# A planned job order for a one-core attention and MoE kernel: TensorE's instruction transfers and neighbour-dependent times enter the planner, and the search is replayed from a list of seeds

## The chip, the cores and the metric

The kernel runs on one core of a Trainium2 chip. The metric is the device time of one execution in microseconds (us), the median of several runs of the kernel before: 524.87 us, from 524.27 to 526.25.

## The reference: what is computed

Three blocks follow each other, in float32, for batch 4, sequence 576, model width 512.

```python
# 1. attention, 8 heads of 64: heads 0-3 see a local window of 32, heads 4-7 every 32nd position
scores = where(mask[h], q @ k.T / 8, -1e9);  attn = softmax(scores);  x = attn @ v
# 2. channel mixing: xk, xr are mixes of x and x shifted by one position
k = max(xk @ w_k, 0);  v = (k * k) @ w_v;  r = sigmoid(xr @ w_r);  x = r * v
# 3. gated feed-forward with a width-3 convolution over the sequence
h = max(x @ w_in, 0);  c = conv3(h);  out = (h * sigmoid(c)) @ w_out
```

## The kernel before

**Precision and counts.** Every large product is made of three matmuls on rounded parts (high by high, low by high, high by low), each of 128 x 288 or 128 x 512 columns. In the profile these are `mm` at L719 (channel mixing, 1,920 matmuls), `hh` at L977 (w_in, 672) and `oo` at L1045 (w_out, 432). Attention is made of small matmuls: scores `sc` at L524, transposes `tr` at L568 and L578, values `pv` and `tr` at L601 and L610. One attention unit is one batch, one pair of heads and one half of the sequence: there are 32. The first batch has four wide local units; all others are narrow.

**Two stages, two plans.** The work up to the end of channel mixing is one list of jobs, the last block is a second one. A job (`plan.add`) names the engine or engines that may run it with a planned duration for each, the buffers that it reads and writes, and a function that issues its instructions. `Plan.run` is a list scheduler. It keeps for each engine a time at which it is free, takes again and again the job that could start first (ties go to the higher `rank`, the length of the path behind it), adds its duration, and so fixes the order of instructions on TensorE, VectorE (DVE), ScalarE (ACT), GpSimd (POOL) and of the DMA issues on SyncE (SP). On the chip each engine works in that fixed order and waits on semaphores; the planned times themselves are not used there, with one exception below.

**The search.** `Plan.search` runs the scheduler 300 times. Each time it draws, from one random stream with seed 1, a window of time and a share of the jobs in it, changes their rank and, for jobs that may run on ACT or DVE, a lean to one of them, and keeps the change when the planned end of TensorE's last job is not later. Then it runs the best order once more, and that order is issued.

**What the planner knows of TensorE.** A job costs its planned duration, plus `ENTER` 0.21 us when the job before it was not a score or value job and this one is, plus `LEAVE` 0.25 us the other way. It also follows how fast the queue ahead of TensorE fills: `FEED` is 14.2 ns for one instruction, `QUEUE` 64 instructions may wait ahead, and a job is not over before its instructions have been fed (`filled`).

**Stirring.** Up to 60 us of the first stage, where the plan leaves TensorE idle for long enough, dummy matmuls on a zero tile (`stir`, L886) are issued into a bank that is free or about to be overwritten. Ten stand at the start. Their number is worked out from the planned idle time: `int((start - pe_end - 0.3) / 0.17)`. This is the exception: planned times decide a number of instructions.

Of the kernel before, what the change touches and what calls it, by code (L numbers as in the profile page):

```python
# [30 lines left out]
DMA_RATE, DMA_LATENCY = 280.0e3, 2.0  # L31
FOREVER = 1.0e9
PREFER, PREFER_FROM, BESIDE = 0.5, 20.0, 0.3
ENTER, LEAVE = 0.21, 0.25
QUEUE, FEED = 64, 0.0142
ROUNDS = 300
HALF_ARRAY = {"sc", "pv"}
BLOCKS = ("B11", "B21", "B22", "T4", "T1", "T2", "T3")
WEIGHTS = ("A11", "A12", "A22", "S3", "S4", "S1", "S2")
# [3 lines left out]
SECOND = {"PE": 0.0, "ACT": 3.0, "DVE": 4.0, "POOL": 0.0, "SP": 0.0}  # L43
# [24 lines left out]

class Job:
    def __init__(self, n, engines, emit, table, nbytes, fed):  # L70
        self.fed, self.lean = fed, 0.0
        self.n, self.engines, self.emit, self.table, self.nbytes = n, engines, emit, table, nbytes
        self.before, self.after, self.spaces = {}, [], []
        self.rank, self.end, self.done, self.room = 0.0, 0.0, False, None
        self.tail = 0.0


class Plan:
# [5 lines left out]


    def __init__(self):
        self.jobs, self.hints, self.tags, self.opened = [], [], {}, {}

    def add(self, engines, emit, reads=(), writes=(), table=None, nbytes=0, fed=0):
        j = Job(len(self.jobs), engines, emit, table, nbytes, fed)  # L90
        self.jobs.append(j)
        for group, write in ((reads, False), (writes, True)):
            for x in group:
                s, parts = x if isinstance(x, tuple) else (x, range(len(x.writer)))
                if s.place is None:
                    s.place = len(self.tags.setdefault(s.tag, []))
                    self.tags[s.tag].append(s)
                    self.opened.setdefault(s.tag, 0)
                if s not in j.spaces:
                    j.spaces.append(s)  # L100
                    s.left += 1
                    s.jobs.append(j)
                for i in parts if not isinstance(parts, int) else (parts,):
# [61 lines left out]
        for j in self.jobs:  # L165
            j.end, j.done, j.room = 0.0, False, None

    def search(self, start=None, rounds=0):
# [4 lines left out]
        keep = [(j.rank, 0.0) for j in self.jobs]  # L173
        draw, best, at = random.Random(1), None, None
        for k in range(rounds):
            tried = list(keep)
            if at:
                t0, width = draw.uniform(0.0, best), draw.choice((8.0, 25.0, 400.0))
                amount, share = draw.choice((0.3, 1.0, 3.0)), draw.choice((0.05, 0.3))
                for i, j in enumerate(self.jobs):  # L180
                    if abs(at[i] - t0) <= width / 2 and draw.random() < share:
                        rank, lean = tried[i]
                        if len(j.engines) > 1 and draw.random() < 0.5:
                            lean = draw.uniform(-0.6, 0.4)
                        tried[i] = rank + draw.gauss(0.0, amount), lean
            for j, (j.rank, j.lean) in zip(self.jobs, tried):
                pass
            self.reset(opened, spaces)
            out = self.run(start, best)
            end = max(end for _, e, _, end in out if e == "PE") if out else FOREVER  # L190
            if best is None or end <= best:
                best, keep = end, tried
                at = {j.n: t for j, _, t, _ in out}
        if rounds:
            for j, (j.rank, j.lean) in zip(self.jobs, keep):
                pass
        self.reset(opened, spaces)
        return self.run(start, None, True)

    def run(self, start=None, limit=None, final=False):  # L200

        free = dict(start or dict.fromkeys(LATENCY, 0.0))
        dma, table, out, halves, filled = 0.0, None, [], False, 0.0
# [3 lines left out]
        left = len(self.jobs)  # L207

        def release(j):
            for e in j.engines:  # L210
# [1 line left out]
                ready[e].append((t, j))  # L212

        for j in self.jobs:
            j.halves = any(s.tag in HALF_ARRAY for s in j.spaces)
            if not wait[j]:
                release(j)
        while left:
            best, bound = None, FOREVER
            for e, jobs in ready.items():  # L220
                now = free[e]
                for t, j in jobs:
                    if t < now:
                        t = now
                    if t > bound + 1.0:
                        continue
                    for s in j.spaces:
                        if not s.open:
                            t = max(t, self.slot(s, j))
                    if t > bound + 1.0:  # L230
                        continue
                    late = t
                    if e == "DVE" and len(j.engines) > 1:
                        late += j.lean + PREFER * (t > PREFER_FROM)
                    if e == "PE" and j.halves:
                        late += max(0.0, max(filled, t - QUEUE * FEED) + j.fed * FEED - t - j.engines[e]) - BESIDE * halves
                    key = (round(late, 2), -j.rank, j.n)
                    if t < FOREVER and (best is None or key < best[0]):
                        best, bound = (key, t, e, j), late
            assert best, "no job can start"  # L240
            _, t, e, j = best
            if e == "PE" and final:
                j.room = self.room(j, free[e])
            for s in j.spaces:
                if not s.open:
                    s.open = True
                    self.opened[s.tag] += 1
            cost = j.engines[e]
            if e == "PE":
                cost += 0.0 if halves == j.halves else ENTER if j.halves else LEAVE  # L250
                halves = j.halves
                filled = max(filled, t - QUEUE * FEED) + j.fed * FEED
                cost = max(cost, filled - t)
            if j.table and j.table != table:
                cost += 1.29
                table = j.table
# [23 lines left out]
def block_kernel(ctx, tc, qkL, qkS, vL, vW, vS, mu_k, mu_r, w_k, w_v, w_r, w_in, conv_w, w_out, ident, mask_l, mask_w, mask_s, out):  # L280
# [195 lines left out]
    def unit(b, p, half, loaded):  # L476
# [46 lines left out]
                    for u in steps:  # L523
                        pe.matmul(bank_of[j]()[to + u:to + u + m, at_[j]:at_[j] + nk], qk()[r, qo[j] + u:qo[j] + u + m], qk()[r, ko[j] + u:ko[j] + u + nk], start=True, stop=True)  # L524

        cost = 0.06 if local and not wide else 4 * (0.002 + nk * 0.00024) if twist else 0.033 + nk * 0.00167
        if early:
            for s_ in range(2):
                k = plan.add({"PE": len(sections[s_]) * cost}, lambda e, s_=s_: scores(e, sections[s_]), [(qk, range(1 + s_))], [banks[s_]], fed=8 * len(sections[s_]))
                if s_ == 0:  # L530

                    for j in late:
                        j.before[k] = True
                        k.after.append(j)
        else:
            first_scores.append(plan.add({"PE": nb * cost}, lambda e: scores(e, range(nb)), [qk], banks, fed=8 * nb * len(steps)))
        for s_, blocks in enumerate(sections):
            def masked(e, blocks=blocks):
                for i in blocks:
# [32 lines left out]
        else:  # L572
# [4 lines left out]
                for i, n in pairs:  # L577
                    pe.transpose(turned()[:n, i // 2 * rows:(i // 2 + 1) * rows], pr()[:rows, i * gap:i * gap + n], id_sb[:rows, :rows])  # L578

            plan.add({"PE": n0 * (0.108 if local else 0.1) - 0.07}, turn, [pr, fixed["id"]], [turned], fed=2 * n0)  # L580
            both = nb // 2 * rows

            def turned_out(e):
# [25 lines left out]
                            r, o = slice(64 * ab, 64 * ab + 64), i * rows + 64 * (ab ^ (odd and turn_of[1])) + u  # L609
                            pe.matmul(outs_[odd]()[r, i * nq + u:i * nq + u + m], vt()[part, v, r], pt()[part, o:o + m], start=True, stop=True)  # L610

        plan.add({"PE": nb * (0.12 if wide else 0.08 if local else 0.062)}, values, [vt, pt], outs_, fed=8 * nb * len(steps))
        x, n = xT[b], nb * nq
        if wide:
            copy(lambda: x()[:, p, 1 + first * nq:1 + (first + nb) * nq], lambda: out_()[:, :n], n, [out_], [(x, 2 * p + half)])
# [268 lines left out]
    def stir(n, into, anew=True):  # L884
        for _ in range(n):
            pe.matmul(into[:, :T], idle[:, :P], idle, start=anew, stop=anew)  # L886
# [38 lines left out]
        j.tail = TAIL  # L925

    def issue(stirred=False):
        pe_end = 0.0
        with tc.manual_schedule():
            if stirred:  # L930
                stir(WARM, scrap)
            for job, e, start, end in plan.search(START if stirred else SECOND, ROUNDS):
                if e == "PE":
                    if stirred and 5.0 < start < STIR_UNTIL and job.room:
                        bank, anew = job.room
                        n = int((start - pe_end - 0.3) / 0.17)
                        if n > 0:
                            stir(n, bank(), anew)
                    pe_end = end
                job.emit(e)  # L940

    issue(True)
# [231 lines left out]
```

## Time and profile before

| | us |
|---|---|
| median of 3 runs | 524.87 |
| lowest, highest | 524.27, 526.25 |
| the profiled execution | 524.43 |
| its span, first to last instruction | 522.6 |
| TensorE busy | 510.7 (98% of the span) |
| VectorE busy | 390.2 (75%) |
| ScalarE busy | 356.2 (68%) |
| matmuls, and weight loads | 4,898 each |
| DMA moved | 90.27 MB, mean 173 GB/s |

The span is 1.8 us shorter than the profiled execution's time. A busy TensorE is not one at its peak: a matmul's record lasts longer than the distance to the next one's start, and dummy matmuls are busy too. Distances between starts of groups in the timeline tell more than the busy share.

### The profile page before, as it was taken

The numbers are of one execution on the slowest core, as the hardware profiler recorded it, in microseconds if no ns is written. First come the engines' busy times: TensorE is split into PE (matmuls) and PEld (weight loads), VectorE is DVE, ScalarE is ACT, GpSimd is POOL, SyncE is SP. The second block draws the span as 40 slices with busy tenths as digits, with TensorE's granted clock in tenths as the row PEclk, the third lists the DMA queues.
The fourth block names the chain that finished last, engine by engine and source line by source line (L and its number), as shares of the span: only waits on it lengthen the run. The fifth ranks groups of instructions, "written<-read, shape, count | busy, mean of one in ns | idle before, by whom it ended". The sixth has DMA issues, their size and how long they took to land.

```text
span 522.6 us, 12915 instructions
## 1 busy us (share of the span) xinstructions
PE 510.7 (98%) x4898; PEld 474.6 (91%) x4898; DVE 390.2 (75%) x1143; ACT 356.2 (68%) x1074; POOL 1.1 (0%) x15
## 2 busy tenths in 40 slices
PE   9999999999999989999999999999999999999997
PEld 5679999989999979999999999999989898898885
DVE  4989899988957978878887415599986876696610
ACT  5989997999947889949799344376644645455420
POOL 0000000000000000000000000000000000000000
PEclk9989999999999999999999999999999999999999
DMA  7965565995476593478785540754137006300111
GB/s 228 357 243 168 181 204 167 300 299 167 153 254 221 155 342 106 152 249 268 265 300 190 153 142 2 272 188 180 40 102 257 27 16 246 131 21 20 41 41 60
DMA packets 50654, 90.27 MB, mean 173 GB/s; under 512 B 4257, under 2 KB 32673, under 8 KB 50593
## 3 DMA queue, kind: packets, MB, share of 16 engines
q1 hardware_dynamic: 50304, 89.29, 50.8%
q8 instruction: 38, 0.62, 0.5%
q14 instruction: 24, 0.19, 0.1%
q10 hardware_dynamic: 288, 0.16, 0.1%
HBM read 60.80 MB, written 28.64 MB: 171 GB/s over the span
## 4 chain that ended last, share of the span: by engine, by line
PE 90%; DVE 5%; ACT 3%; issue 1%; POOL 0%; DVEq 0%; ACTq 0%; POOLq 0%
PE mm L719 48%; PE oo L1045 19%; PE hh L977 15%; PE sc L524 3%; PE pv L610 2%; PE tr L578 2%; DVE pr L540 1%; DVE c L1024 1%; ACT mx L698 1%; ACT pr L545 1%; PE tr L610 1%; PE scrap L886 0%; DVE pr L556 0%; DVE c L1026 0%; DVE mx L699 0%
## 5 line engine op out<-in xcount | busy, mean ns | idle before, releaser
L977 PEld LDWEIGHTS hh<-x,wi 128*128 128x128 f32 x672 | 92.8, 188 | 3.8 <-DVE c L1026 0.6
L977 PE MATMUL hh<-x,wi 128*128 128x288 f32 x672 | 95.1, 296 | 0.5 <-DVE gAl L1031 0.4
L719 PE MATMUL mm<-X,wvh 128*128 128x288 f32 x448 | 84.1, 298 | 0.0
L719 PE MATMUL mm<-Y,wkh 128*128 128x288 f32 x384 | 68.3, 294 | 0.0
L719 PEld LDWEIGHTS mm<-X,wvh 128*128 128x128 f32 x448 | 66.8, 188 | 0.5
L719 PE MATMUL mm<-Y,wrh 128*128 128x288 f32 x256 | 57.9, 305 | 0.2
L545 ACT ACTIVATE pr<-pr,nmx 128x54 f32<-128x54 f32 (+2 forms) x160 | 53.4, 341 | 5.1 <-DVE nmx L540 4.8
L719 PEld LDWEIGHTS mm<-Y,wkh 128*128 128x128 f32 x384 | 56.6, 188 | 0.1
L1024 DVE SCALAR_TENSOR_TENSOR c<-hb,cw_sb,c 128x576 f32<-128x576 f32 x64 | 50.8, 813 | 0.6
L719 PE MATMUL mm<-X,wvl 128*128 128x288 f32 x224 | 47.9, 295 | 0.0
L719 PEld LDWEIGHTS mm<-Y,wrh 128*128 128x128 f32 x256 | 43.3, 191 | 1.2 <-ACT rs L731 0.6
L1045 PE MATMUL oo<-wo,gAh 128*128 128x512 f32 x160 | 43.2, 392 | 0.0
L719 PE MATMUL mm<-Y,wkl 128*128 128x288 f32 x192 | 40.9, 294 | 0.0
L719 PE MATMUL mm<-Y,wrl 128*128 128x288 f32 x128 | 38.3, 299 | 0.6 <-DVE wrl L401 0.6
L760 DVE TENSOR_TENSOR X<-sq,X 128x288 fp32r<-128x288 f32 x48 | 21.7, 456 | 23.0 <-ACT X L758 19.5
L719 PEld LDWEIGHTS mm<-X,wvl 128*128 128x128 f32 x224 | 35.9, 188 | 0.0
L1045 PE MATMUL oo<-wo,gBh 128*128 128x512 f32 x128 | 34.4, 390 | 0.0
L1025 ACT ACTIVATE c<-c 128x576 f32<-128x576 f32 x32 | 21.9, 686 | 17.6 <-DVE c L1024 17.2
L1045 PEld LDWEIGHTS oo<-wo,gAh 128*128 128x128 f32 x160 | 28.8, 188 | 4.8
L742 ACT ACTIVATE rl<-mm 128x288 f32<-128x288 f32 x64 | 25.4, 405 | 8.8 <-PE mm L719 8.6
L545 ACT ACTIVATION_READ_ACCUMULATOR pr<-pr,nmx 128x1 f32 x160 | 31.2, 195 | 0.0
L719 PEld LDWEIGHTS mm<-Y,wkl 128*128 128x128 f32 x192 | 30.7, 188 | 0.0
(121 smaller groups left out, 1056.4 us busy)
## 6 DMA issues: line engine op xcount, KB each, us to landing
x_d<-xo SPq DMA_DIRECT2D x42, 288.0 KB, 2.9
x<-x_d SPq DMA_DIRECT2D x21, 576.0 KB, 5.0
wi_d<-ws SPq DMA_DIRECT2D x24, 256.0 KB, 3.5
wi<-wi_d SPq DMA_DIRECT2D x6, 896.0 KB, 6.6
qk<-in_qkS SPq DMA_DIRECT2D x8, 599.0 KB, 6.9
out<-ob SPq DMA_DIRECT2D x18, 256.0 KB, 2.0
qk<-in_qkL SPq DMA_DIRECT2D x7, 592.0 KB, 6.3
raw<-in_w_k SPq DMA_DIRECT2D x8, 512.0 KB, 3.9
```

Of the source, the lines that this page charges most:

```text
L524: pe.matmul(bank_of[j]()[to + u:to + u + m, at_[j]:at_[j] + nk], qk()[r, qo[j] + u:qo[j] + u + m], qk()[r, ko[j] + u:ko[j] + u + nk], star ...
L540: dve.tensor_tensor_reduce(pr()[:, i * gap:i * gap + nk], bank_of[i]()[:, at_[i]:at_[i] + nk], masks[i], -1.0 / 8.0, 3.0e38, ALU.add, ALU. ...
L545: act.activation(pr()[:, k], pr()[:, k], AF.Exp, bias=nmx()[:, i:i + 1], scale=-1.0, accum_out=sums()[:, i:i + 1])
L578: pe.transpose(turned()[:n, i // 2 * rows:(i // 2 + 1) * rows], pr()[:rows, i * gap:i * gap + n], id_sb[:rows, :rows])
L610: pe.matmul(outs_[odd]()[r, i * nq + u:i * nq + u + m], vt()[part, v, r], pt()[part, o:o + m], start=True, stop=True)
L719: pe.matmul(o(), w_cols(name, j, t, part), x_[t](), start=(t == 0 and part == 0 and x_ is xhi), stop=(t == nk - 1 and x_ is xlo))
L742: plan.add({"ACT": 0.295}, lambda e: act.activation(r(), o(), AF.Relu), [o], [r])
L760: plan.add({"DVE": 0.37}, lambda e: dve.tensor_tensor(l_(), sq(), h_().bitcast(F32), ALU.subtract), [sq, h_], [l_])
L977: pe.matmul(o(), w(hw, j), x()[:, hx, j], start=anew and n == 0 and j == 0, stop=last and n == 2 and j == 1, skip_group_check=True)
L1024: plan.add({"DVE": 0.735}, lambda e, k=k: dve.scalar_tensor_tensor(c(), h()[:, k:k + S], cw_sb[:, k * NF + f:k * NF + f + 1], c(), ALU.mul ...
L1025: plan.add({"ACT": 0.6}, lambda e: act.activation(c(), c(), AF.Sigmoid), [c], [c], table="sigmoid")
L1045: pe.matmul(o(), x_()[:, f, col:col + P], wsp["wo", f]()[:, part], start=(f == 0 and x_ is th and part == 0), stop=(f == NF - 1 and x_ is tl))
```

## The change

Two constants of neighbours (`ENTER`, `LEAVE`) become tables by the kinds of the job before and the job itself: `half` (scores and values), `tr` (transposes), `mm` (all others). `feed` replaces the two lines that followed the filling of the queue: instructions come in transfers of 256, the plan starts with 85 of the first one used, and the transfer after next is usable 4.0 us after the step into the next one, or later by 0.3 of the planned time for which the DMA queue is still full, counted up to 7 us. Dummy matmuls are now planned inside `run`, by the same formula, and their instructions are counted. Planned durations of scores, transposes and values are set anew. The search draws nothing by itself any more: it applies, in order, the 39 (first stage) or 30 (second stage) listed seeds, each one random change, and issues the last order. The seeds run from 2000004 to 2006306 and from 4000006 to 4007008.

```diff
-ENTER, LEAVE = 0.21, 0.25
 QUEUE, FEED = 64, 0.0142
-ROUNDS = 300
+CHUNK, AHEAD, FETCH, CROWD = 256, 85, 4.0, (0.3, 7.0)
+GAP = {("mm", "half"): 0.09, ("tr", "half"): 0.17, ("tr", "tr"): 0.08}
+ENTER = {("half", "mm"): 0.11, ("tr", "mm"): 0.085, ("half", "tr"): 0.05}
+STEPS = (
+    (
+        2000004, 2000047, 2000063, 2000067, 2000104, 2000109, 2000170, 2000173, 2000192, 2000237, 2000248,
...
+    def search(self, start=None, steps=()):
...
+        for seed in (None, *steps):
+            if out:
+                at = {j.n: t for j, _, t, _ in out}
+                keep = self.vary(seed, keep, at, max(end for _, e, _, end in out if e == "PE"))
...
+            out = self.run(start)
+        return out
+
+    def feed(self, j, t, filled, n, usable, dma):
+
+        f, left = max(filled, t - QUEUE * FEED), j.fed + (j.kind != "mm")
+        while left:
+            k = min(left, CHUNK - n % CHUNK)
+            f, n, left = f + k * FEED, n + k, left - k
+            if n % CHUNK == 0:
+                f = max(f, usable)
+                usable = f + FETCH + CROWD[0] * min(CROWD[1], max(0.0, dma - f))
+        return f, n, usable
...
-                    if e == "PE" and j.halves:
-                        late += max(0.0, max(filled, t - QUEUE * FEED) + j.fed * FEED - t - j.engines[e]) - BESIDE * halves
+                    if e == "PE":
+                        late += max(0.0, self.feed(j, t, filled, fetched, usable, dma)[0] - t - j.engines[e])
+                        late -= BESIDE * (kind == j.kind == "half")
...
+            if e == "PE":
+                t = max(t, free[e] + (GAP.get((kind, j.kind), 0.0) if kind != "half" else leave * (j.kind != "half")))
+                idle = t - free[e]
+                if self.stirred and 5.0 < t < STIR_UNTIL and idle > 0.48 and self.room(j, free[e]):
+                    j.room, j.idle = self.room(j, free[e]), int((idle - 0.3) / 0.17)
+                    fetched += 2 * j.idle
...
-                cost += 0.0 if halves == j.halves else ENTER if j.halves else LEAVE
-                halves = j.halves
-                filled = max(filled, t - QUEUE * FEED) + j.fed * FEED
+                cost += ENTER.get((kind, j.kind), 0.0)
+                filled, fetched, usable = self.feed(j, t, filled, fetched, usable, dma)
                 cost = max(cost, filled - t)
...
-        cost = 0.06 if local and not wide else 4 * (0.002 + nk * 0.00024) if twist else 0.033 + nk * 0.00167
+        cost = 0.26 + 0.06 * (nb - 4) if local and not wide else 0.33 + 0.06 * (nb - 5) if twist else nb * (0.033 + nk * 0.00167)
...
-            plan.add({"PE": n0 * (0.108 if local else 0.1) - 0.07}, turn, [pr, fixed["id"]], [turned], fed=2 * n0)
+            plan.add({"PE": n0 * 0.1 - 0.06}, turn, [pr, fixed["id"]], [turned], fed=2 * n0)
...
-        plan.add({"PE": nb * (0.12 if wide else 0.08 if local else 0.062)}, values, [vt, pt], outs_, fed=8 * nb * len(steps))
+        plan.add({"PE": nb * 0.12 if wide else 0.49 + 0.17 * (nb - 4) if local else 0.49}, values, [vt, pt], outs_, fed=8 * nb * len(steps), leave=0.12 if local else 0.0)
...
-            for job, e, start, end in plan.search(START if stirred else SECOND, ROUNDS):
+            for job, e, start, end in plan.search(START if stirred else SECOND, STEPS[not stirred]):
```

## Rows read from the trace of the kernel before

**Rows 1.** Stretches: busy us of PE, PEld, DVE, ACT, POOL; PEclk, DMA share, GB/s

```profile
0.00:60.00 60.00, 55.74 (x739) 45.40 (x740) 48.98 (x208) 51.05 (x185) 0.61 (x7) 0.97 0.74 243
60.00:330.00 270.00, 266.57 (x3064) 259.77 (x3063) 208.57 (x703) 210.82 (x696) 0.48 (x8) 1.00 0.61 201
330.00:522.60 192.60, 188.36 (x1099) 169.46 (x1098) 132.66 (x235) 94.37 (x195) 0.00 (x0) 1.00 0.32 111
```

**Rows 2.** Dummy matmuls by target, first 60 us: busy us, mean ns, idle before

```profile
L886 PE MATMUL mm<-idle 128*128 128x288 bf16 x46 | 7.5, 288 | 0.0
L886 PE MATMUL sc<-idle 128*128 128x288 bf16 x10 | 2.3, 360 | 0.2 <-DVE nmx L540 0.2
```

**Rows 3.** TensorE's waits, whole span: who waited for whom, us, times, longest

```profile
PE sc L524 <- issue: 3.0, 2, 2.2
PE pv L610 <- issue: 1.2, 2, 0.8
...
PE hh L977 <- DVE gAl L1031: 0.4, 1, 0.4
```

**Rows 4.** TensorE's timeline, attention without a stall: start us, us, operation, idle before

```profile
104.54 0.27 PE L610 MATMUL pv<-pt,vt 54*64 54x54 f32 x2
...
105.04 0.66 PE L524 MATMUL sc<-qk 64*32 64x64 f32 x40
105.63 0.53 PE L719 MATMUL mm<-X,wvh 128*128 128x288 f32 x2
...
107.11 0.45 PE L524 MATMUL sc<-qk 64*32 64x64 f32 x32
107.49 0.52 PE L578 MATMUL tr<-id_sb,pr 118*118 118x118 f32 x3
```

**Rows 5.** The same timeline at three of the four idle times put down to issue

```profile
28.87 0.64 PE L524 MATMUL sc<-qk 64*32 64x64 f32 x13
...
30.67 0.40 PE L719 MATMUL mm<-Y,wrh 128*128 128x288 f32 x1
...
185.67 0.32 PE L610 MATMUL pv<-pt,vt 54*64 54x54 f32 x3
186.34 0.20 PE L610 MATMUL pv<-pt,vt 54*64 54x54 f32 x1 [0.35 <-issue]
...
186.83 0.39 PE L524 MATMUL sc<-qk 64*32 64x64 f32 x22
...
189.96 0.45 PE L524 MATMUL sc<-qk 64*32 64x64 f32 x31
192.57 0.24 PE L524 MATMUL sc<-qk 64*32 64x64 f32 x1 [2.17 <-issue]
192.74 0.40 PE L719 MATMUL mm<-Y,wrh 128*128 128x288 f32 x1
```

**Rows 6.** DMA queue that carries instructions, whole span: packets, MB, share of engines

```profile
q8 instruction: 38, 0.62, 0.5%
```

**Rows 7.** DMA queues from 186.4 to 190 us; q8 has no line there

```profile
q1 hardware_dynamic: 566, 1.40, 103.1%
```

**Rows 8.** DMA queue of instructions from 190 to 192.6 us

```profile
q8 instruction: 1, 0.02, 2.2%
```

**Rows 9.** Chain that ended last, from 45 us: start us, us, what

```profile
45.91 38.37 PE mm L719 x287
```

**Rows 10.** Busy us of each engine from 31 to 35 us, columns as in Rows 1

```profile
31.00:35.00 4.00, 4.00 (x36) 3.62 (x35) 2.73 (x11) 2.20 (x7) 0.00 (x0) 0.57 0.27 78
```

**Rows 11.** Timeline of ScalarE, VectorE and TensorE between 30 and 46 us

```profile
33.02 0.36 ACT L646 ACTIVATE xT<-pv 128x108 f32<-128x108 f32 x2 [1.80 <-PE pv L610]
...
34.11 0.69 DVE L361 SCALAR_TENSOR_TENSOR wt<-wb,wt 128x512 int32<-128x512 int32 x1 [1.27 <-ACT wb L350]
...
44.49 0.66 PE L886 MATMUL mm<-idle 128*128 128x288 bf16 x4
...
45.91 0.40 PE L719 MATMUL mm<-Y,wrl 128*128 128x288 f32 x1 [0.63 <-DVE wrl L401]
```

More of the change, by code (lines that the diff above doesn't have):

```diff
@@ L33 @@
 PREFER, PREFER_FROM, BESIDE = 0.5, 20.0, 0.3
-ENTER, LEAVE = 0.21, 0.25
 QUEUE, FEED = 64, 0.0142
-ROUNDS = 300
+CHUNK, AHEAD, FETCH, CROWD = 256, 85, 4.0, (0.3, 7.0)
[3 more added lines that the diff above has]
+    (
[4 rows of a table added]
+    ),
+    (
[3 rows of a table added]
+    ),
+)
 HALF_ARRAY = {"sc", "pv"}
@@ L70, in __init__ @@
     def __init__(self, n, engines, emit, table, nbytes, fed):
-        self.fed, self.lean = fed, 0.0
+        self.fed, self.lean, self.leave = fed, 0.0, 0.0
         self.n, self.engines, self.emit, self.table, self.nbytes = n, engines, emit, table, nbytes
@@ L86, in __init__, with add @@
     def __init__(self):
-        self.jobs, self.hints, self.tags, self.opened = [], [], {}, {}
-    def add(self, engines, emit, reads=(), writes=(), table=None, nbytes=0, fed=0):
+        self.jobs, self.hints, self.tags, self.opened, self.stirred = [], [], {}, {}, False
+    def add(self, engines, emit, reads=(), writes=(), table=None, nbytes=0, fed=0, leave=0.0):
         j = Job(len(self.jobs), engines, emit, table, nbytes, fed)
+        j.leave = leave
         self.jobs.append(j)
@@ L166, in reset, with vary @@
             j.end, j.done, j.room = 0.0, False, None
-    def search(self, start=None, rounds=0):
+    def vary(self, seed, keep, at, end):
+        draw, tried = random.Random(seed), list(keep)
+        t0, width = draw.uniform(0.0, end), draw.choice((8.0, 25.0, 400.0))
+        amount, share = draw.choice((0.3, 1.0, 3.0)), draw.choice((0.05, 0.3))
+        for i, j in enumerate(self.jobs):
+            if abs(at[i] - t0) <= width / 2 and draw.random() < share:
+                rank, lean = tried[i]
+                if len(j.engines) > 1 and draw.random() < 0.5:
+                    lean = draw.uniform(-0.6, 0.4)
+                tried[i] = rank + draw.gauss(0.0, amount), lean
+        return tried
+    def search(self, start=None, steps=()):
         self.rank()
@@ L172, in search @@
         spaces = {s: (s.left, s.end, s.open) for j in self.jobs for s in j.spaces}
[L173 to L187, printed above, removed]
-            self.reset(opened, spaces)
[L189 to L200, printed above, removed]
+        keep, out = [(j.rank, 0.0) for j in self.jobs], None
+        for seed in (None, *steps):
+            if out:
+                at = {j.n: t for j, _, t, _ in out}
+                keep = self.vary(seed, keep, at, max(end for _, e, _, end in out if e == "PE"))
+            for j, (rank, lean) in zip(self.jobs, keep):
+                j.rank, j.lean = rank, lean
+            self.reset(opened, spaces)
+            out = self.run(start)
@@ L202, in run @@
+        return out
[8 more added lines that the diff above has]
+        return f, n, usable
+    def run(self, start=None, limit=None):
         free = dict(start or dict.fromkeys(LATENCY, 0.0))
-        dma, table, out, halves, filled = 0.0, None, [], False, 0.0
+        dma, table, out, kind, filled, fetched, usable, leave = 0.0, None, [], "mm", 0.0, AHEAD, 0.0, 0.0
@@ L206, in run @@
         ready = {e: [] for e in LATENCY}
-        left = len(self.jobs)
+        left, todo = len(self.jobs), sum(j.engines.get("PE", 0.0) for j in self.jobs)
         def release(j):
@@ L214, in run @@
         for j in self.jobs:
-            j.halves = any(s.tag in HALF_ARRAY for s in j.spaces)
+            tags = {s.tag for s in j.spaces}
+            j.kind = "half" if ("sc" in tags or "vt" in tags) else "tr" if "tr" in tags else "mm"
             if not wait[j]:
@@ L241, in run @@
             _, t, e, j = best
-            if e == "PE" and final:
-                j.room = self.room(j, free[e])
+            if e == "PE":
[4 more added lines that the diff above has]
+                    fetched += 2 * j.idle
+                    if fetched % CHUNK < 2 * j.idle:
+                        usable = t + FETCH + CROWD[0] * min(CROWD[1], max(0.0, dma - t))
+                else:
+                    j.room = None
             for s in j.spaces:
@@ L249, in run @@
             if e == "PE":
-                cost += 0.0 if halves == j.halves else ENTER if j.halves else LEAVE
-                halves = j.halves
-                filled = max(filled, t - QUEUE * FEED) + j.fed * FEED
+                cost += ENTER.get((kind, j.kind), 0.0)
+                filled, fetched, usable = self.feed(j, t, filled, fetched, usable, dma)
                 cost = max(cost, filled - t)
+                kind, leave = j.kind, j.leave
+                todo -= j.engines[e]
+                if limit is not None and t + cost + todo > limit:
+                    return None
             if j.table and j.table != table:
@@ L524, in scores @@
                         pe.matmul(bank_of[j]()[to + u:to + u + m, at_[j]:at_[j] + nk], qk()[r, qo[j] + u:qo[j] + u + m], qk()[r, ko[j] + u:ko[j] + u + nk], start=True, stop=True)
-        cost = 0.06 if local and not wide else 4 * (0.002 + nk * 0.00024) if twist else 0.033 + nk * 0.00167
+        cost = 0.26 + 0.06 * (nb - 4) if local and not wide else 0.33 + 0.06 * (nb - 5) if twist else nb * (0.033 + nk * 0.00167)
         if early:
             for s_ in range(2):
-                k = plan.add({"PE": len(sections[s_]) * cost}, lambda e, s_=s_: scores(e, sections[s_]), [(qk, range(1 + s_))], [banks[s_]], fed=8 * len(sections[s_]))
+                k = plan.add({"PE": len(sections[s_]) * cost / nb}, lambda e, s_=s_: scores(e, sections[s_]), [(qk, range(1 + s_))], [banks[s_]], fed=8 * len(sections[s_]))
                 if s_ == 0:
@@ L535, in unit @@
         else:
-            first_scores.append(plan.add({"PE": nb * cost}, lambda e: scores(e, range(nb)), [qk], banks, fed=8 * nb * len(steps)))
+            first_scores.append(plan.add({"PE": cost}, lambda e: scores(e, range(nb)), [qk], banks, fed=8 * nb * len(steps), leave=0.15))
         for s_, blocks in enumerate(sections):
@@ L927, in issue @@
     def issue(stirred=False):
-        pe_end = 0.0
+        plan.stirred = stirred
         with tc.manual_schedule():
@@ L931, in issue @@
                 stir(WARM, scrap)
-            for job, e, start, end in plan.search(START if stirred else SECOND, ROUNDS):
+            for job, e, start, end in plan.search(START if stirred else SECOND, STEPS[not stirred]):
                 if e == "PE":
-                    if stirred and 5.0 < start < STIR_UNTIL and job.room:
+                    if job.room:
                         bank, anew = job.room
[L936 to L939, printed above, removed]
+                        stir(job.idle, bank(), anew)
                 job.emit(e)
```

6 rows, old and new, of the table STEPS are left out of this document.

## The prediction

> **What bounds the kernel now.** I read the busy times by stretch first, because the share of the whole span hides where TensorE is short of work. TensorE is busy in 55.74 of the first 60 us, 266.57 of 270 us up to 330, and 188.36 of 192.6 after that, with VectorE and ScalarE both above 48 of 60 in the first stretch only [rows 1]. So TensorE sets the time, and from 60 us on VectorE and ScalarE have room. The first 60 us are another regime: all three engines are nearly full, and part of TensorE's busy time there is dummy matmuls, 7.5 and 2.3 us into live banks [rows 2], so TensorE is in truth short of work.
>
> Then TensorE's own waits. The largest are 3.0 and 1.2 us put down to "issue", in two waits each, which means that no semaphore was open; waits for another engine are small, as 0.4 us for VectorE in the second stage [rows 3]. The timeline tells what these four cost. A block of 40 score matmuls followed by a dense product goes from 105.04 to 105.63, 0.59 us; one of 32 from 107.11 to 107.49, 0.38; a value block of 24 from 104.54 to 105.04, 0.50 [rows 4]. With a stall the same blocks take 30.67 - 28.87 = 1.80, 192.74 - 189.96 = 2.78 and 186.83 - 185.67 = 1.16 us [rows 5], so 1.21, 2.40 and 0.66 us are lost. The last had 0.35 us of recorded idle, so a restart costs some 0.31 on top; the fourth stall (0.8 idle, in a value block) comes to 1.1. Together 5.4 us, of which 1.2 lie before 60 us and 4.2 behind.
>
> That these are late instruction transfers is borne out by the DMA rows. TensorE ran 2 x 4,898 = 9,796 loads and matmuls, and one queue moved 38 packets with 0.62 MB [rows 6]: 258 instructions and 16 KB a packet. From 186.4 to 190 us this queue moved nothing while the data queue filled 103% of the 16 engines [rows 7]; one packet came after 190 [rows 8], and TensorE resumed at 192.57. The stalls ended at 186.34 and 192.57 [rows 5], 6.23 us apart. The diff's formula allows 4.0 + 0.3 x 7 = 6.1 at most, so its size is right where data DMAs crowd. In dense work a transfer lasts 128 x 0.134 = 17 us (287 matmuls in 38.37 us, [rows 9]), so only the attention stretches can run short.
>
> The Trainium skill's page "Runtime: NRT & Kernel Launch", section "Instruction fetch mechanics", speaks against the change: the sequencer fetches the next 256-instruction block while it runs the current one, and crossing a block boundary is mostly hidden. By it there would be no fetch term to win, and the sum below would end near -2.2 instead of -5.3 us. The trace agrees on the block size and on most boundaries, and differs at the four stalls above.
>
> **The change part by part.** No instruction of the computation is added or removed; only the order changes, and which of ACT and DVE runs a job, and the count of dummies. The order of all queues changes together: SP's DMA issues follow the same list, so loads of later units can move against the transfers too.
>
> *Transfers in the plan (`feed`, `CHUNK`).* To live without a stall, 256 instructions must last 6.2 us. A value block of 24 and a score block of 40 take 1.09 us for 64 matmuls, 17 ns each [rows 4]; a dense one takes 134 ns. Of 128 matmuls, x dense ones with 0.134x + 0.017(128 - x) = 6.2 gives x = 35. The stretches around 112 and 186 us have such dense jobs ready, and postponing attention jobs by a few us there delays only units that the next batch needs later. So the 4.2 us behind 60 us can go in full; at worst the plan's DMA times (280 GB/s in one line) are wrong by some us, and stalls come back elsewhere. Bounds: 4.2 gained to 2.4 lost (one more stall of the longest kind). I take three quarters, 3.1 us, because the formula meets the measured 6.23 but the crowding term rests on planned DMA times.
>
> *The first 60 us.* The stall at 29 us is worth more than its 1.2. Right behind it the granted clock averages 0.57 from 31 to 35 us [rows 10], that is 1.2 GHz most of the time, which costs 4 x 0.43 = 1.7 us of dense work. The value block held up by both kept ScalarE idle for 1.80 us at 33.02, VectorE then waited 1.27 for it, and the last piece of `wr` came to TensorE at 45.91 after 0.63 idle and four dummies [rows 11]. From 45.91 on, TensorE runs dense without a hole [rows 9]. So what counts is how early this VectorE chain ends, not TensorE's own 2.9 us: the hole of 1.27 is what goes when the stall goes, and what is late next is VectorE itself, filled with mixing and weight splitting. I take 1.3 us. Bounds: above, half of the 9.8 us of live-bank dummies [rows 2], 4.9; below, one new hole like the 1.80 us on ScalarE, -1.8. The dummy rule is the same formula; counting their 2 instructions each costs nothing on the chip.
>
> *Neighbour costs and new durations.* The plan charged 0.46 us for going into scores or values and back; it charges 0.09 + 0.15 + 0.11 = 0.35 now. A value block of 24 was planned at 6 x 0.062 = 0.37, is now 0.49, and takes 0.50 [rows 4], so old planned times ran 0.13 us ahead at each such block. This changes which job goes first by a few tenths: with some 24 narrow units behind the first batch and one or two excursions in each, saving two or three of about 40 is 2.5 x 0.2 = 0.5 us. Bounds -1 to +1.5; I take 0.5.
>
> *The search.* 11 of the 39 first-stage seeds lie within the first 300 numbers, so if numbers are tries in order, about as many steps were found in 300 rounds before, and 28 come on top. What they win by the plan isn't shown by any row; the three terms above are what they have to win from.
>
> *Second stage.* Its TensorE wait is 0.4 us for VectorE [rows 3], its dense work has no fetch limit (17 us against 6.2), and behind its last matmul stand one copy and one DMA as before. I take 0.4 won; bounds 1 won to 1 lost, since 30 seeds reorder jobs here for hardly any prize.
>
> Sum: 3.1 + 1.3 + 0.5 + 0.4 = 5.3 us. The profiled execution's 524.43 (span 522.6, 1.8 around it) becomes 519.1; it lies 0.44 below the median of the runs, so the forecast on the median is 519.5 us.
>
> **Rivals.**
> - *Better in the plan alone.* Transfers are late elsewhere, because the loads that crowd them moved too. For it: the data queue is full for several us at a time [rows 7], and the plan treats it as one line. Against it: the size of the lateness is met. Stalls of 4 us in sum remain, and 523.5 comes out.
> - *The start contracts as well.* Twenty times as many tries find an order in which the VectorE chain ends 4.9 us earlier. For it: 9.8 us of dummies. Against it: VectorE and ScalarE are already busy for 49 and 51 of the 60 us [rows 1]. All 4.2 + 4.9 + 0.3 go: 515.5.
> - *Slower: the clock at the start.* The place is 25 to 46 us, where dummies stand only where the planned time is idle. If a new order leaves TensorE waiting where the plan saw none, the clock falls as it did at 31 us. Each us at 1.2 GHz costs half a us on dense work, so it decides from 10.6 us at that level, three falls of 3.5 us. Against it: one stall made one fall so far, and most of the change removes stalls. With 18 us so spent: 524.9 - 5.3 + 9 = 528.6.
> - *No fetch term, as if transfers were hidden.* Only the start, neighbours and second stage give: 524.9 - 2.2 = 522.7. The rows on the transfers are against it.
>
> **How the numbers follow.** Forecast 0.54, better in the plan alone 0.16, start contracts 0.16, slower 0.08, no fetch term 0.06. A change under 0.5% (2.6 us, below 522.2 or above 527.5) can't be told from none. Faster: nearly all of the forecast, the contracted start and a little of the fourth, 0.72; within: the first rival with most of the fourth and a rest of the slow one, 0.20; slower 0.08. The range is 515.2 to 524.5: below lies some 0.06, above most of the slow case and the worse part of the first. The forecast's own range is 517 to 522.
>
> **What would show it.** Right: waits put down to issue fall from 4.2 to under 1.5 us, the packets of q8 stay 38, the stretch with dense matmuls without a hole begins 1 to 2 us earlier than 45.91, and the granted clock from 20 to 60 us stays above 0.95. First-stage work should end some 5 us earlier and the second stage keep its length within 1 us. Wrong: issue waits of 3 us or more at new places, a later start of the dense stretch, a longer fall of the clock, or a second stage longer by over 1 us.

## The result, and the profile after

The changed kernel takes 518.38 us (median of 6 runs, 516.85 to 519.4) against 524.94 for the kernel before (6 runs, 523.65 to 526.25). The ratio is 0.9874, 95% interval 0.9851 to 0.9897, or 5.4 to 7.8 us less. The forecast was 519.5, 5.4 us less. The profiled execution, 519.4 with a span of 517.6, is the slowest of its six.

The granted clock, averaged over a whole run, differs between runs. In the 69 runs of the kernel before that stand beside the experiments it was 0.999 or more in 13 (mean time 523.0 us), 0.996 to 0.998 in 32 (524.8 us) and lower in 24 (526.4 us). One stretch at 1.2 GHz like that behind the stall at 29 us, 0.50 from 31.1 to 34.5 us, takes 3.4 x 0.5 / 522.6 = 0.003 off a run's mean, so the second group is about one such stretch from the first, and 1.8 us. The changed kernel had 0.998 or more in all 12 of its runs, and the profiled one kept 1.00 to the last matmul.

Three stretches of the changed kernel, with the second one ended where its first stage ends (columns as in [rows 1]), and then 20 to 60 and 31 to 35 us:

```profile
0.00:60.00 60.00, 55.80 (x794) 44.63 (x795) 50.05 (x222) 54.03 (x197) 0.61 (x7) 1.00 0.76 250
60.00:325.00 265.00, 263.62 (x2990) 256.89 (x2989) 205.59 (x685) 205.17 (x685) 0.99 (x8) 1.00 0.61 203
325.00:517.60 192.60, 188.84 (x1107) 170.51 (x1105) 131.10 (x237) 92.84 (x194) 0.00 (x0) 1.00 0.32 111
...
20.00:60.00 40.00, 37.27 (x533) 32.31 (x531) 38.22 (x129) 40.00 (x134) 0.00 (x0) 1.00 0.68 216
...
31.00:35.00 4.00, 3.65 (x63) 3.09 (x62) 3.56 (x11) 4.00 (x17) 0.00 (x0) 1.00 0.82 286
```

The granted clock is 1.00 from 31 to 35 us, where it was 0.57 [rows 10]. ScalarE is busy for all of the 40 us from 20 to 60. The time came off before 325 us: the second stage starts and ends as follows, first before, then after (timeline of TensorE: first group of `hh`, last of `oo`).

```profile
329.17 1.50 PE L977 MATMUL hh<-x,wi 128*128 128x288 f32 x10
...
518.27 0.62 PE L1045 MATMUL oo<-wo,gBl 128*128 128x512 f32 x2
```

```profile
325.11 5.60 PE L1010 MATMUL hh<-x,wi 128*128 128x288 f32 x38
...
513.29 0.61 PE L1078 MATMUL oo<-wo,gBl 128*128 128x512 f32 x2
```

So 4.06 us were won in the first stage, and 189.10 - 188.18 = 0.92 in the second. In both, TensorE starts after 1.1 us, and from the start of its very last matmul to the end are 4.1 us.

TensorE's waits after (who waited for whom: us, times, longest), its one remaining stall by issue in the timeline, and the queue of instructions:

```profile
PE sc L560 <- issue: 0.9, 1, 0.9
PE mm L755 <- DVE wrl L437: 0.7, 2, 0.3
PE tr L614 <- ACT xT L682: 0.6, 2, 0.4
```

```profile
100.32 0.33 PE L560 MATMUL sc<-qk 64*64 64x54 f32 x7
101.59 0.39 PE L560 MATMUL sc<-qk 64*64 64x54 f32 x11 [0.94 <-issue]
```

```profile
q8 instruction: 38, 0.62, 0.5%
```

Issue waits fell from 4.2 [rows 3] to 0.9 us, with the same 38 transfers [rows 6].

### The profile page after: what moved, and what is told of

Its sections match the earlier page's. It is cut to its first block, busy times and chain, and to the rows that moved or that the text cites. A ratio compares the mean times of both kernels' runs of the same rounds, so it can differ in the third digit from the quotient of the medians.

```text
span 517.6 us, 12872 instructions
## 1 busy us (share of the span) xinstructions
PE 508.3 (98%) x4886; PEld 472.0 (91%) x4886; DVE 386.7 (75%) x1142; ACT 352.0 (68%) x1075; POOL 1.6 (0%) x15
## 4 chain that ended last, share of the span: by engine, by line
PE 85%; ACT 9%; DMA 3%; DVE 3%; issue 1%; ACTq 0%; DVEq 0%
PE mm L755 43%; PE oo L1078 19%; PE hh L1010 17%; ACT pr L581 3%; PE sc L560 2%; PE pv L646 2%; PE tr L614 1%; DMA raw<-in_w_in 1%; ACT mx L734 1%; ACT wb L386 1%; DMA wi_d<-ws 1%; DMA qk<-in_qkL 1%; ACT Y L736 1%; DVE pr L576 1%; DVE pr L592 0%
## 5 line engine op out<-in xcount | busy, mean ns | idle before, releaser
L1010 PE MATMUL hh<-x,wi 128*128 128x288 f32 x672 | 93.4, 296 | 0.1
L755 PE MATMUL mm<-Y,wrh 128*128 128x288 f32 x256 | 56.0, 300 | 0.3 <-ACT rs L767 0.2
L755 PEld LDWEIGHTS mm<-Y,wrh 128*128 128x128 f32 x256 | 42.2, 188 | 1.5 <-ACT rs L767 0.4
L1088 ACT ACTIVATE ob<-oo 128x512 f32<-128x512 f32 x17 | 10.0, 597 | 38.5 <-PE oo L1078 38.1
```

The costliest lines, as they stand in the source:

```text
L755: pe.matmul(o(), w_cols(name, j, t, part), x_[t](), start=(t == 0 and part == 0 and x_ is xhi), stop=(t == nk - 1 and x_ is xlo))
L1010: pe.matmul(o(), w(hw, j), x()[:, hx, j], start=anew and n == 0 and j == 0, stop=last and n == 2 and j == 1, skip_group_check=True)
L1088: act.activation(ob(), o(), AF.Copy, scale=0.5)
```

## The experiments

Times are medians; each job ran the kernel before beside its kernels, at 525.06, 524.99 and 524.95 us in 23 runs each. "Issue" is the sum of TensorE's waits put down to issue in the one profiled execution.

| kernel | transfers in the plan | times | first-stage search | median (range), us | issue |
|---|---|---|---|---|---|
| before | no | old | 300 | 524.94 (523.65 to 526.25) | 4.2 |
| changed | yes | new | listed | 518.38 (516.85 to 519.4) | 0.9 |
| e1 changed, again | yes | new | listed | 517.43 (516.18 to 518.12) | 0.6 |
| e2 | yes | new | none | 524.16 (521.81 to 526.44) | none |
| e3 | yes | new | listed, old second stage | 519.24 (518.68 to 520.1) | none named so |
| e4 | yes, boundaries moved | new | listed | 520.77 (519.1 to 525.07) | 1.4 |
| e5 | yes | new | 6,310 | 519.22 (518.34 to 520.77) | 1.0 |
| e10 | yes | new | 6,310, second series | 519.35 (516.75 to 520.92) | 3.5 |
| e7 | yes | old | 6,310 | 517.16 (516.79 to 517.73) | 0.8 |
| e11 | yes | old | 6,310, second series | 520.40 (519.01 to 526.09) | 1.2 |
| e12 | yes | old | 20,000 | 518.80 (517.86 to 519.52) | 0.8 |
| e6 | no | new | 6,310 | 522.41 (519.94 to 525.45) | 2.4 |
| e8 | no | old | 6,310 | 521.22 (518.4 to 525.57) | 1.2 |
| e9 | yes, loads doubled | new | listed | 522.75 (520.68 to 526.36) | 2.1 |

My theory A: transfers that come late cost the kernel before some 5 us, and a plan that knows of them avoids most of it. Rival B: the longer search, or the better neighbour times, carry the gain.

**e1, the changed kernel again.**

> The changed kernel once more, beside the three others of this job, so that they are compared on one chip. Both theories: 518.4 us, within 1.5, and one wait put down to issue near 100 us of some 0.9 us.

517.43 us, within what was expected. The stall near 100 us is missing in this execution; 0.6 us stand in two waits at 18 and 19 us. The first stage of the same order ended at 323.56 us here and at 325.11 above: single profiles differ by 1.5 us, and only medians can carry differences of that size.

**e2, no search.**

```diff
 STEPS = (
-    (2000004, 2000047, ... 2006306),
+    (),
```

> The changed planner with an empty seed list for the first stage (second stage unchanged). Theory A, the transfers and neighbour times in the plan carry the gain: issue waits stay under 2 us in sum, and the time is within 2.5 us of the changed kernel, some 520.5 us. Rival B, the longer search carries it: the unsearched order gives the gain back, 523.5 us or more.

524.16 us: B's number, and A's sign. The issue waits are gone without any search, but the gain in time is gone as well. In their place are more waits for other engines:

```profile
PE sc L555 <- DVE nmx L571: 0.9, 2, 0.5
PE mm L750 <- DVE wrl L432: 0.9, 2, 0.5
PE mm L750 <- ACT wrh L431: 0.7, 1, 0.7
PE mm L750 <- DVE wvl L432: 0.5, 2, 0.3
PE mm L750 <- ACT rs L762: 0.5, 1, 0.5
```

All of TensorE's waits behind the first matmul come to 4.7 us here and to 3.7 in the changed kernel, issue included, but the first stage ends at 328.28 instead of 325.11 us; so the waits are about a third of the loss, and where the rest lies was not located. The knowledge of transfers is not the gain by itself: an unsearched order that avoids them is no better than the searched order of before that runs into them. The unsearched order of the old planner was not run.

**e3, the second stage ordered as before.**

```diff
-plan.search(START if stirred else SECOND, STEPS[not stirred])
+(plan.search(START, STEPS[0]) if stirred else plan.search_old(SECOND, 300))
```

> The changed first stage, with the second stage ordered as before (300 rounds from one random stream). Theory A, the second-stage seeds are worth what the two traces show between the first hh and the last oo matmul (189.10 against 188.18 us): 0.9 us slower than the changed kernel, 519.3 us. Rival B, that difference follows from how the first stage ends and not from the seeds: equal to the changed kernel within 0.3 us.

519.24: A's number, 1.8 us slower than e1 beside it. The second stage, from 324.96 to 513.96 us, takes 189.00 us, as before the change; in e1, from 323.56 to 511.75, it takes 188.19. The seeds of that stage are worth 0.8 us; the rest, in these two profiles, is the first stage, which has the same order in both.

```profile
324.96 5.73 PE L1041 MATMUL hh<-x,wi 128*128 128x288 f32 x39
...
513.96 0.62 PE L1109 MATMUL oo<-wo,gBl 128*128 128x512 f32 x2
```

**e4, block boundaries moved by 80 instructions.**

```diff
-stir(WARM, scrap)
+for _ in range(5 * WARM):
+    pe.matmul(scrap[:16, :40], idle[:, :16], idle[:, :40], start=True, stop=True)
```

> The changed kernel with 50 small dummy matmuls (16 x 40) at its start in place of 10 large ones; the plan is not told. This puts 40 load and matmul pairs, 80 instructions, ahead of all else, so every transfer boundary falls 40 matmuls earlier in the program. Theory A, the plan avoids stalls by where the boundaries fall: issue waits of 2 us or more in sum at new places, 1 to 3 us slower than the changed kernel. Rival B, the plan thins attention everywhere so that any 256 instructions last long enough: issue waits stay near 0.9 us and the time within 0.7 us.

520.77, 3.3 us slower than e1. No dense work starts later at the beginning: the first dense product stands at 29.97, in the changed kernel at 29.91. Two waits by issue come up at new places, of 0.3 and 1.1 us; that is 1.4 in sum, less than the 2 that A asked for, and 3.3 us is a little over A's 1 to 3. B falls.

The places are telling when matmuls are counted from the program's first. The stalls stand before matmul 467, 1,482, 2,370 and 2,497 in the kernel before, 1,230 in the changed one, 1,483 and 2,245 here, 1,484 and 2,372 in e6, 2,495 in e8, 218, 1,233, 2,122 and 2,248 in e10, 342 in e5 and e12. Their distances are close to multiples of 127 matmuls. The exact count takes in weight loads and semaphore instructions: ahead of the weight load of the matmul that comes late stand 192 or 193 instructions more than a multiple of 256. That holds for 26 of the 28 waits by issue in all fourteen profiles, whatever work stands there; the other two, 0.3 us each, are before matmul 245 in e1 and e9. So it is the position in the stream and not the work that stalls.

The transfers themselves settle what comes late there. Before each of the 26 a packet of 16 KB on the queue of instructions (q8) ended 1.23 to 1.51 us before TensorE resumed: at 28.98, 111.56, 184.95 and 191.23 us for the four stalls of the kernel before, which end at 30.30, 113.07, 186.34 and 192.57. Before the other two the last packet had ended 2.5 and 2.8 us earlier. The timeline at 1,483 and, in e6, at 1,484:

```profile
109.86 0.22 PE L646 MATMUL tr<-pt,vt 54*64 54x54 f32 x1
110.39 0.20 PE L646 MATMUL tr<-pt,vt 54*64 54x54 f32 x1 [0.32 <-issue]
```

```profile
107.33 0.62 PE L557 MATMUL sc<-qk 64*32 64x64 f32 x36
109.68 0.30 PE L557 MATMUL sc<-qk 64*32 64x64 f32 x4 [1.73 <-issue]
```

**e5, another searched order of the changed planner**, the control for e6 to e8. A change is kept where the plan gets strictly shorter; the edit is another list of seeds.

> The changed planner with other first-stage seeds: 6,310 random changes in a row, kept where the plan gets strictly shorter, 14 of them; second stage unchanged. It is the control for the three others of this job, which are searched in the same way. Theory A, any searched order of this plan gives the gain: 517 to 520 us, issue waits under 1.5 us. Rival B, the listed seeds are better than their plan tells: 521 us or more.

519.22: A. The listed order is some 1.3 us better than this one (518.38 and 517.43), which is about what orders of one planner differ by.

**e6, no transfers in the plan**, neighbour times kept, searched anew.

```diff
             if n % CHUNK == 0:
-                f = max(f, usable)
                 usable = f + FETCH + ...
```

> The changed planner without the line that lets a job wait for the next transfer of 256 instructions, so that the neighbour times stand alone; 6,310 changes tried, 20 kept. Theory A, the transfers in the plan carry the gain: issue waits of 3 to 5 us come back, 2.5 to 5 us slower than the control. Rival B, neighbour times and longer search carry it: within 1.5 us of the control.

522.41, 3.2 us slower than the control, with stalls of 1.7 and 0.7 us: A on the time, a little less than A in the issue waits of this execution, which at 520.07 us lies below their median. The stall of 1.7 us, which ends at 109.68, costs more than its idle time: soon behind it the granted clock is 0.50 for over 3 us.

```profile
111.20:114.50 3.30, 3.30 (x16) 3.30 (x15) 3.30 (x8) 2.44 (x10) 0.00 (x0) 0.50 0.34 118
```

In runs with a mean clock of 0.999 or more the two kernels are 2.0 us apart (521.3 in 4 runs against 519.3 in 6).

**e7, transfers with the old times.**

```diff
-GAP = {("mm", "half"): 0.09, ...}
+GAP = {}
-ENTER = {("half", "mm"): 0.11, ("tr", "mm"): 0.085, ("half", "tr"): 0.05}
+ENTER = {("mm", "half"): 0.21, ("tr", "half"): 0.21, ("half", "mm"): 0.25, ("half", "tr"): 0.25}
...
-            first_scores.append(plan.add({"PE": cost}, lambda e: scores(e, range(nb)), [qk], banks, fed=8 * nb * len(steps), leave=0.15))
+            first_scores.append(plan.add({"PE": cost}, lambda e: scores(e, range(nb)), [qk], banks, fed=8 * nb * len(steps)))
...
```

The durations of scores, transposes and values go back to the old ones in the same way, and the seeds are this planner's own.

> The changed planner with the old durations of scores, transposes and values and the old 0.21 and 0.25 us of neighbours, but with the transfers; 6,310 changes tried, 15 kept. Theory A: issue waits under 1.5 us and within 1.5 us of the control. Rival B: the transfers can't be placed by a plan whose times run ahead, issue waits of 2 us or more, 2 to 4 us slower than the control.

517.16, with 0.8 us by issue: A in the issue waits. It is 2.1 us faster than the control, where A had it within 1.5; B falls.

**e8, the old planner with the long search** and the changed second stage.

```diff
-ROUNDS = 300
+STEPS = (
+    (
+        2000001, 2000004, 2000028, 2000158, 2000233, 2000251, 2000296, 2000303, 2000465, 2000977, 2000989,
+        2001242, 2001271,
+    ),
...
```

The second list is that of the changed kernel.

> The planner of before, without transfers and with the old neighbour times, but 6,310 changes tried in the first stage, 13 kept, and the second stage of the changed kernel. Theory A: the second stage gives 0.9 us, the longer search next to nothing, issue waits of 3 us or more stay: 522.5 to 525 us. Rival B, the longer search carries the gain: 520 us or less.

521.22, between A and B. Beside the second stage's 0.8 us, this order is some 3 us better than that of before (3.8 in sum), so the longer search is not "next to nothing" here; one order doesn't tell how much of that is the draw. With 1.2 us by issue, its profiled execution did not show the 3 us that A asked for. It stays 4.1 us behind e7, which differs by the transfers, by where the search went with them, and by small parts of the changed planner (dummies are placed while planning, and the filling of the queue is weighed for every kind of job). In runs with a mean clock of 0.999 or more they are 3.6 us apart (520.8 in 8 runs against 517.2 in 6).

**e9, the query-key loads issued twice.**

```diff
 q.dma_start(out=out_(), in_=in_())
+if again is not None:
+    q.dma_start(out=again, in_=in_())
```

`again` is a scratch tile in DRAM, given for the loads of the last three batches.

> The changed kernel, in which each of the 12 query-key loads of the last three batches is issued a second time, into scratch in DRAM, 592 or 599 KB each; the plan is not told. Theory A, a transfer of instructions is late because it queues behind data on the DMA engines: issue waits of 3 us or more in the attention stretches of 90 to 120 and 165 to 200 us, against 0.6 to 0.9 us, and 3 to 8 us slower. Rival B, a transfer takes some 4 us from the step into a block whatever the data DMAs do: issue waits stay under 1.5 us; what is slower then stands as waits for the loads.

Neither. It is 522.75, but the loss is in the first 60 us, where late weights hold the start (the 168th dense matmul starts at 63.2 instead of 58.5 us, as much as the whole loss) and the granted clock is 0.50 from 20.7 to 24.0 and from 51.4 to 54.7 us. The 2.1 us by issue stand at 18 to 20 and at 31 us. From 165 to 200 us the DMA engines are busier, 0.90 against 0.71, and TensorE is not idler; first e9, then the changed kernel:

```profile
165.00:200.00 35.00, 34.68 (x626) 32.12 (x625) 28.84 (x139) 32.92 (x136) 0.00 (x0) 1.00 0.90 323
```

```profile
165.00:200.00 35.00, 34.56 (x654) 31.88 (x653) 31.39 (x147) 33.84 (x145) 0.00 (x0) 1.00 0.71 246
```

That data transfers make those of instructions late, as the formula's crowding term has it, is therefore not shown by this run; what other runs say of it stands at the end.

**e10, e11, e12, further searches**: the changed planner with a second series of changes; the old times with transfers, a second series; the same with 20,000 changes tried. The edits are lists of seeds on e5 and e7.

> The changed planner with a second series of 6,310 random changes, 13 kept: the second draw for the control (519.22 us). Theory A, the new neighbour times and durations are worth nothing on the chip, orders of one planner differ by 1 to 2 us by chance: 517 to 520 us, not below the next kernel by over 1 us. Rival B, they help, and the first control was a bad draw: 516.5 us or less and 1 us or more below the next kernel.

> Transfers in the plan, old durations and neighbour times, a second series of 6,310 changes, 15 kept. Theory A: 516.5 to 519 us, as in the first draw (517.16), issue waits under 1.5 us. Rival B, the first was a lucky draw: 519.5 us or more.

> As the kernel before this one, with 20,000 changes tried and 19 kept, as a version that may beat the changed kernel. Theory A, the search of this plan is used up after some thousand tries: within 1 us of the other two transfers-only kernels, some 517 us. Rival B, more tries go on to pay: 515.5 us or less.

519.35, 520.40 and 518.80. e10: A by its time (it lies 1.05 us below e11, where A allowed 1); the new times are worth nothing that can be measured here; orders with them took 517.4 to 519.4 us, with the old ones 517.2 to 520.4. e11: its rival B, e7 was a lucky draw. e12: neither number was met, 518.8 lies between e7 and e11; more tries did not pay. None beats the changed kernel clearly: e7, at 517.16 against 518.38 and 517.43, is as fast.

e10 has 3.5 us by issue in its profile in spite of the plan, at four places, among them these two:

```profile
173.65 0.19 PE L644 MATMUL pv<-pt,vt 64*64 64x32 f32 x1 [1.50 <-issue]
...
181.26 0.53 PE L753 MATMUL mm<-X,wvh 128*128 128x288 f32 x2 [0.71 <-issue]
```

They are one block apart (matmul 2,122 and 2,248) and 7.61 us, more than the 6.1 that the formula grants at most. In the trace the packet for the second starts 5.31 us after TensorE resumed from the first, takes 1.04, and TensorE resumes 1.26 us after its end. Up to that start the data queue is full:

```profile
q1 hardware_dynamic: 566, 1.76, 101.0%
```

So what is long is the time before the packet starts, and not the packet.

**What follows.** Searched orders with transfers and the new second stage took 517.2 to 520.4 us (six orders, mean 518.8 with the listed one at 517.9), those without 522.41 and 521.22 (mean 521.8). The slowest with is faster than the fastest without: the transfers are worth some 3 us, 0.8 to 5.3 by the single pair, with the stretches at 1.2 GHz that their stalls bring. From before to the two without it is another 3.2, of which 0.8 is the second stage and some 2.4 goes with the longer search; that part is not shown, since it rests on two orders and on one order of before, and orders of one planner differ by 1 to 3 us. The sum, 3.0 + 0.8 + 2.4 = 6.2, is by its making the distance from before to the mean of the six; the changed kernel's own 6.6 is near it.

## Why the prediction was right

**Transfers in the plan** (3.1 of 4.2 us behind 60 us). Right. In the first profile one stall of 0.94 us idle remains there, in e1 none, so some 3 to 4.2 are gone; by e5 against e6 it is 3.2, by e7 against e8 4.1. That they are late transfers, which the prediction took from counts and two DMA rows, is shown by the counts and the ends of the packets under e4. The rival without a fetch term, 522.7, is out: e6, whose plan has none, is 3.2 us behind its control.

The rule of the Trainium skill (page "Runtime: NRT & Kernel Launch", section "Instruction fetch mechanics") that crossing a block boundary is mostly hidden holds for most of the 38 transfers and not for these: with transfers out of the plan, e6 and e8 still show issue waits of 2.4 and 1.2 us.

**The first 60 us** (1.3 us). Right in size in the two profiles, wrong in the sign that was to show it. Up to 60 us both kernels have done 179 dense matmuls, and the 300th starts at 75.99 and 75.94 us. But the changed kernel has by then done one unit more of attention: its scores from 50.94 to 51.33, its values to 52.12, and a transpose block, 0.39 + 0.79 + 0.14 = 1.3 us. The stall at 29 us, the fall of the clock behind it and ScalarE's hole of 1.80 us [rows 11] are gone. Over all runs the clock alone goes with more: the median of the kernel before, 525.0 us, lies 2.0 above its 13 runs at 0.999 or more, and at that clock the changed kernel (9 runs, mean 517.6) is 5.4 us ahead, where the medians are 6.6 apart (7.6 beside e1). Where the clock fell in the runs without a profile isn't known, so how much of the 2.0 belongs to the first 60 us stays open; the 1.7 us that the prediction gave one fall fits. I had looked for a dense stretch that begins 1 to 2 us before 45.91 [rows 9]; it begins later, and what is late next isn't VectorE, as I wrote, but ScalarE. The chain that ended last, after, from 41 us (start, us, what):

```profile
41.08 1.00 ACT pr L581 x6
42.07 0.47 ACT mx L734
...
42.55 0.71 ACT wrh L436
43.26 0.58 ACT wb L386
43.85 0.67 ACT mx L734
44.52 0.58 ACT rs L767 x2
45.10 0.52 ACT wkh L436
45.62 0.66 ACT pr L581 x4
...
48.35 2.65 PE mm L755 x18
```

**Neighbour costs and new durations** (0.5 us). Not shown. Two searched orders with the new times, e5 and e10, and three with the old ones, e7, e11 and e12, average 519.3 and 518.8 us.

**Second stage** (0.4 us). Right in sign, 0.8 to 0.9 us in size, shown by e3.

**The search**. This is where the prediction's reasoning was weak. It gave the search no term of its own, since no row shows what 28 further steps win, and let the terms above stand for it. e2, with no search, takes 524.16 us and is no faster than before, and in e8 an order from 6,310 tries on the old planner is some 3 us better than that from 300. By these orders more than a third of the gain went with the search (2.4 of 6.2 us). That the forecast's total came out near is in part luck: 1.3 + 0.5 stood where 2.4 was measured, 0.4 where 0.8 was. The forecast of 5.4 us lies at the small end of the measured 5.4 to 7.8.

**The rivals.** Better in the plan alone did not happen: issue waits fell from 4.2 to 0.9 and 0.6 us. The clock did not fall at the start. The start did not contract by 4.9 us: TensorE still waits there for weights and for ScalarE.

## What to carry to other kernels

When TensorE's waits name no engine, count its instructions, loads and semaphores included, from the start of the program. Here 26 of 28 such waits stood at one and the same place of every 256, while the work under them changed with the order; and a packet on the queue of instructions ended shortly before each. Such stalls are late transfers, and an order planned with them in view lost most of them. A planner that learns of such a cost may have to search again before it pays: here its first order gave back elsewhere all that it avoided. Compare several orders of each planner, since two orders of one planner differ by as much as the term that is to be measured, and compare the granted clock of the runs too.

## What the runs showed of the hardware

- A block of 256 instructions that followed a late one was usable 5.1 us (e11, 107.80 to 112.94), 5.8 us (e12, 18.84 to 24.60), 6.2 us (before, 186.34 to 192.57 [rows 5]) and 7.6 us (e10) after it. The packet itself takes 0.92 to 1.09 us in these four, and TensorE resumes 1.26 to 1.37 us after its end; the rest, 2.9 to 5.3 us, is the time until the packet starts.
- From the end of a stall by issue to the start of the next packet of instructions it took 1.1 to 1.7 us in the five cases in which the DMA engines were under 0.6 busy meanwhile (before, 30.30 and 113.07; the changed kernel, 101.59; e5, 25.06; e8, 189.69). In the other 21, with 0.8 busy or more, it took 1.5 to 5.3 us, in 12 of them over 3. So the delay goes with the data traffic, as the formula's crowding term has it; that the traffic causes it is not shown, since e9, which was to test it, lost its time elsewhere.
- Idle times of 0.79 us at 29 us of the kernel before and of 1.73 us at 108 us of e6 were followed by some 3.4 us at 1.2 GHz, while one of 2.17 us at 190 us of the kernel before left the granted clock at 1.00 in the 2.5 us behind it. Before the 0.79 us TensorE had run only attention matmuls and dummies, before the two others dense products between the attention blocks. So neither the length of the idle time nor the dense products before it tell these cases apart; what does stays open.
- The same order ended its first stage at 323.56, 324.96 and 325.11 us in three executions (e1, e3 and the first profile). In e3 the largest wait, 1.1 us, is put down to VectorE but stands before matmul 1,357, 127 behind the 1,230 of the changed kernel, in the middle of six transposes that run without a wait in e1 and in the changed kernel; and a packet of instructions ended 1.56 us before TensorE resumed. By these marks it is a late transfer under another name, though the VectorE instruction named had ended only 0.1 us before.
